# Starting the weight conversion one attention round sooner in a fused attention, SwiGLU and maxout kernel

## The chip, the cores and the metric

The kernel runs on one core of a Trainium2 chip, as one program. The metric is the device time of one execution in microseconds (us). Engine names are those of the profile: PE is TensorE's matmul, PEld its weight load, DVE VectorE, ACT ScalarE, POOL GpSimd, SP SyncE, which here only issues DMAs. A "q" behind an engine (SPq) is its instruction queue.

## What is computed

Three layers follow one another. The first is a causal attention with a decay, over 2 batches, 8 heads, 768 positions and head size 64, in blocks of 64 with a running state:

```
Dmask     = lam ** (i - j)            for i >= j, else 0
intra     = ((qb @ kb.T) * Dmask) @ vb
inter     = (qb * lam ** (i + 1)) @ kv_state
kv_state  = lam ** 64 * kv_state + (kb * lam ** (63 - j)).T @ vb
```

The second layer takes the result as 1536 tokens of 512 features, normalises them (RMS), and computes `(silu(xn @ w_gate) * (xn @ w_val)) @ w_out` with 1536 hidden features. The third computes `maximum(x @ w1, x @ w2, x @ w3) @ w_out2` with 768 hidden features. The weight matrices arrive as 64-bit floats, so every weight is read as two 32-bit words.

## The kernel before, in words

**Weights.** The weights are cut into units of 128 hidden features. `load_to` (L164) loads one unit as raw words: a 512 KB transfer into the tile `wraw`, issued on SP as three DMAs for the gate and value matrices (`crosswise`, L119) and as one for the others. `begin_unit` (L231) then makes two ACT instructions of it: the absolute value of the high words into the tile `W` (L253) and a shift of the low words inside `wraw` (L254). `words_of_unit` (L204) turns these into a 32-bit float with three DVE instructions (L209, L212, L216) and one POOL add (L219). `finish_unit` (L174) splits the result into a high part `wh` (ACT, L180) and a low remainder `wl` (POOL, L183). A product is three matmuls: high by high, low by high, high by low. `W` has three buffers in the pool `wp`, and one more in a later pool for some units of the third layer. `wraw` has three buffers in `wp` and two in the pool `ld`.

**Order of the units.** `unit_list` (L128) begins g0 v0 g1 v1 g2 o0 o1 v2 g3 v3 o2 o3, where g, v and o are gate, value and output matrix and the number is the block of hidden features. These twelve are the units for which there is room while the attention runs.

**Attention.** The 1536 tokens are twelve chunks of 128. Seven rounds s = 0 to 6 (the loop at L985) run the steps of `attn_q` in the order of `orders` (L435). In round s the letter T is `turn` of chunk s (transposes `pk`, `pq`, their copies `kT`, `qT` on ACT, the scaled queries `qs` on DVE, which need `lami`), C is `scores` of chunk s-1 (which needs the decayed keys `kd`, made on POOL from `Tm`), a and b are the masked scores `A` (DVE, from `Tm`), V advances the state `S`, M is `mixed` of chunk s-2 (`px` on PE, then `sq` and `x` on ACT), U sums the squares (`pm` on PE, `ms` on DVE, `ri` on POOL), N applies the norm (`pb`, `x`, `xh`), R makes `xl` (POOL). T also issues the next loads: value of chunk s+1, key and query of chunk s+2 (L104), each 256 KB in pieces of 256 bytes.

Between these steps stand the weights. At the end of rounds 2 to 6 one raw unit is loaded (L1010), and at the end of rounds 3 to 6 one unit is begun (L1012); the round after a unit was begun makes its words, and the round after that finishes it. So when `first_stage` (L649) starts, g0 is finished, v0 and g1 have their words, and v1 has been begun. Everything is in one hand-written order, and every engine works through its own instructions in that order: an ACT instruction that waits for a DMA holds up all ACT instructions behind it.

**After the rounds.** `first_stage` runs the second layer on the first four hidden blocks while the rest of the attention is spread over its gaps. `hidden1` (L614) computes gate and value product of one hidden block for 512 tokens; `out_two` (L631) multiplies two finished hidden blocks with o0 and o1, four output tiles of six matmuls each. In the gaps, `third_of_unit` (L259) carries the unit pipeline on by one third of a unit. When the attention is through, the other hidden blocks and the third layer follow, as sums and differences of products.

**Set-up.** L970 to L981: `diag` is a doubled identity; eight scans make `Tm` (the mask of every head), two copies make `lamh`, and four scans make `lami` (the powers of lambda that scale queries and state).

Of the kernel before, what the change touches and what calls it, by code (L numbers as in the profile page):

```python
# [9 lines left out]
F32 = mybir.dt.float32  # L10
F32R = mybir.dt.float32r
AF = mybir.ActivationFunctionType
ALU = mybir.AluOpType
PSUM = bass.MemoryType.PSUM

I32 = mybir.dt.int32
U32 = mybir.dt.uint32

P = 128
# [7 lines left out]
def tile_decay_attention_swiglu_maxout(  # L27
# [16 lines left out]
    nc = tc.nc  # L44
    B, H, S, D = q.shape
    NT, DM = out.shape
    NP = H // 2
# [5 lines left out]
    C = P // 2  # L53
# [8 lines left out]
    wp = ctx.enter_context(tc.tile_pool(name="wp", bufs=WBUFS))  # L62
    psum = ctx.enter_context(tc.tile_pool(name="psum", bufs=8, space=PSUM))
    att_ctx = ctx.enter_context(ExitStack())
    attc = att_ctx.enter_context(tc.tile_pool(name="attc", bufs=1))
# [3 lines left out]
    lates = []  # L69
# [5 lines left out]
    lam8 = attc.tile([P, H], F32, name="lam8")  # L75
    lamh = attc.tile([P, NP], F32, name="lamh")
    g_sb = attc.tile([P, KD], F32, name="g_sb")
    ones = attc.tile([P, P], F32, name="ones")
    ident = attc.tile([P, P], F32, name="ident")
    zeros = attc.tile([P, P], F32, name="zeros")  # L80
    mhalf = attc.tile([P, 1], F32, name="mhalf")
# [13 lines left out]
    def loads_to(c):  # L95
        while nxt_load[0] <= min(c, NCH):
            n = nxt_load[0]
            if n:
                load(n - 1, 2)
            load(n, 0)  # L100
            load(n, 1)
            nxt_load[0] += 1
# [61 lines left out]
    def load_to(n):  # L164
        while pos["load"] < min(n, len(raw_list)):
            nm, f = raw_list[pos["load"]]
            more = pos["load"] % 5 > 2 and pos["load"] < 3 * PLAIN - 2
            t = (ld if more else wp).tile([P, KD, 2 * P], I32, tag="raw", name="wraw", bufs=2 if more else 3)
            for to, src in crosswise(t, source[nm](f)) if nm in "gv" else [(t, source[nm](f))]:
                nc.sync.dma_start(out=to, in_=src)  # L170
            raws[nm, f] = t
            pos["load"] += 1
# [58 lines left out]
    def begin_unit():  # L231
        if pos["made"] == len(unit_list):
            return
        key = unit_list[pos["made"]]
        at = group_of[key] % 2
        if first_use[key] <= pos["step"] + 6 and at < len(wpools) and (key is None or room[at]):
            pos["made"] += 1
            if key is None:
                stage1.append((None,) * 5)
                return  # L240
            room[at] -= 1
            held[key] = at
            if key[0][0] == "T":
                stage1.append((key, None if second_sum(key) else words[key[0][1], key[1]], at, None, None))
                return
            load_to(pos["raw"] + (3 if pos["half"] else 1))
            pos["raw"] += 1
            t = raws.pop(key).rearrange("p k (f w) -> p (k f) w", w=2)
            lo, hi = t[:, :, 0], t[:, :, 1]
            spare = key[0] in "12" and key[1] % 2  # L250
            W = (lates[0] if spare else wp).tile([P, 512], I32, tag="W", name="W", bufs=1 if spare else 3)
            words[key] = W
            nc.scalar.activation(out=W.bitcast(F32), in_=hi.bitcast(F32), func=AF.Abs)  # L253
            nc.scalar.activation(out=lo, in_=lo.bitcast(U32), func=AF.Copy, scale=2.0 ** -29)  # L254
            stage1.append((key, W, at, lo, hi))
# [87 lines left out]
    last_state = [None]  # L343

    def next_state(c, h, old):
        S_ = att.tile([P, NP, D], F32, tag="S", name="S", bufs=4)
        pS = st[c]["sc"][h][:, HF:].rearrange("p (a e) -> p a e", e=D)
        if old is None:
            nc.vector.tensor_copy(out=S_, in_=pS)
        else:  # L350
            for a in range(NP):
                nc.vector.scalar_tensor_tensor(out=S_[:, a, :], in0=old[:, a, :], scalar=lami[:, a, C - 1:C], in1=pS[:, a, :],
                                               op0=ALU.mult, op1=ALU.add)
        return S_

# [26 lines left out]
    def mixed(c):  # L382
        for part in range(2):
            half_mixed(c, part)
        px = st[c]["px"]
        sq = att.tile([P, NP, P], F32, tag="sq", name="sq", bufs=1)
        x = att.tile([P, NP, P], F32, tag="x", name="x", bufs=3)
        for n in range(2):
            nc.scalar.activation(out=sq[:, 2 * n:2 * n + 2, :], in_=px[n][:, :2, :], func=AF.Square)
        for a in range(NP):  # L390
            nc.scalar.activation(out=x[:, a, :], in_=px[a // 2][:, a % 2, :], func=AF.Copy, scale=g_sb[:, a:a + 1])
        ss = sq
        if c > CPNB:
            ss = att.tile([P, 1, P], F32, tag="ss", name="ss", bufs=1)
            nc.vector.tensor_reduce(out=ss[:, 0, :], in_=sq.rearrange("p a t -> p t a"),
                                    axis=mybir.AxisListType.X, op=ALU.add)
        st[c] = dict(x=x, ss=ss)

    def summed(c):
        d = st[c]  # L400
        pm = bank("pm")
        n = d["ss"].shape[1]
        for a in range(n):
            nc.tensor.matmul(out=pm[:, 0:1], lhsT=d["ss"][:, a, :], rhs=ones[:, 0:1], start=a == 0, stop=a == n - 1)
        ms = att.tile([P, 1], F32, tag="ms", name="ms")
        nc.vector.tensor_scalar(out=ms, in0=pm[:, 0:1], scalar1=1.0 / DM, scalar2=EPS, op0=ALU.mult, op1=ALU.add)
        ri = att.tile([P, 1], F32, tag="ri", name="ri")
        nc.gpsimd.tensor_tensor(out=ri, in0=ms, in1=mhalf, op=ALU.pow)
        d["ri"] = ri

# [546 lines left out]
    with tc.manual_schedule():  # L957
        nc.scalar.dma_start(out=lam8, in_=lam.rearrange("(o h) -> o h", o=1).to_broadcast([P, H]))
        loads_to(0)
        for to, src in crosswise(g_sb, rms_g.rearrange("(a p) -> p a", p=P)):  # L960
            nc.scalar.dma_start(out=to, in_=src)
        make_identity(nc, ident)
        nc.vector.memset(ones, 1.0)
        nc.vector.memset(zeros, 0.0)
        nc.scalar.activation(out=mhalf, in_=zeros[:, 0:1], func=AF.Silu)
        nc.vector.memset(mhalf, -0.5)
        warm = bank("warm")
        for i in range(9):
            nc.tensor.matmul(out=warm[:, 0:P], lhsT=zeros, rhs=zeros, start=True, stop=True)
        nc.vector.tensor_tensor(out=diag, in0=ident[:, :C], in1=ident[:, C:], op=ALU.add)  # L970
        for h in range(H):
            nc.vector.tensor_tensor_scan(
                out=Tm[:, h, :], data0=lam8[:, h:h + 1].to_broadcast([P, C]), data1=diag,
                initial=0.0, op0=ALU.mult, op1=ALU.add)
        for hf in range(2):
            nc.vector.tensor_copy(out=lamh[64 * hf:64 * hf + 64, :],
                                  in_=lam8.rearrange("p (a t) -> p t a", t=2)[64 * hf:64 * hf + 64, hf, :])
        for a in range(NP):
            nc.vector.tensor_tensor_scan(
                out=lami[:, a, :], data0=lamh[:, a:a + 1].to_broadcast([P, C]), data1=zeros[:, :C],  # L980
                initial=1.0, op0=ALU.mult, op1=ALU.add)  # L981
        loads_to(1)
        pos["narrow"] = False
        unit_ = None
        for s_ in range(CPNB + 3):  # L985
            if stage1:
                unit_ = stage1.pop(0)
            while attn_q[0][0] == s_:
                fn = attn_q[0][1]
                attn_step()  # L990
                if unit_ and s_ == CPNB + 2:
                    if fn is named["U"][1]:
                        words_of_unit(3, *added_later)
                    elif fn is named["V"][1]:
                        for n in range(3):
                            words_of_unit(n, *unit_, split_add=True)
                        split_unit.append(unit_)
                        stage2.append(unit_[:3])
                elif unit_ and fn is named["b"][1]:
                    words_of_unit(0, *unit_)  # L1000
                elif unit_ and fn is named["U"][1]:
                    words_of_unit(1, *unit_)
                    if stage2:
                        finish_unit(*stage2.pop(0))
                elif unit_ and fn is named["V"][1]:
                    words_of_unit(2, *unit_, split_add=s_ == CPNB + 1)
                    added_later = unit_
                    stage2.append(unit_[:3])
            if s_ > 1:
                load_to(pos["load"] + 1)  # L1010
            if s_ > 2:
                begin_unit()  # L1012
        finish = first_stage()
        pos["step"] = len(steps)
        second_stage(finish)
# [31 lines left out]
```

## Time and profile before

| | us |
|---|---|
| median of three runs | 548.31 |
| lowest and highest run | 547.35, 548.59 |
| the profiled execution, its own time | 547.73 |
| its span, first to last instruction | 545.9 |
| PE busy | 531.4 |
| DVE, ACT, POOL busy | 374.2, 280.1, 300.9 |

Times of single instructions are counted from the start of the span. In a line of a timeline the first number is the start and the second the length, "x4" the number of merged instructions, and the bracket the idle time of that engine just before, with what ended it. [...]

### The profile page before, as it was taken

The numbers are of one execution on the slowest core, as the hardware profiler recorded it, in microseconds if no ns is written. First come the engines' busy times: TensorE is split into PE (matmuls) and PEld (weight loads), VectorE is DVE, ScalarE is ACT, GpSimd is POOL, SyncE is SP. The second block draws the span as 40 slices with busy tenths as digits, with TensorE's granted clock in tenths as the row PEclk, the third lists the DMA queues.
The fourth block names the chain that finished last, engine by engine and source line by source line (L and its number), as shares of the span: only waits on it lengthen the run. The fifth ranks groups of instructions, "written<-read, shape, count | busy, mean of one in ns | idle before, by whom it ended". The sixth has DMA issues, their size and how long they took to land.

```text
span 545.9 us, 9739 instructions
## 1 busy us (share of the span) xinstructions
PE 531.4 (97%) x3728; PEld 438.8 (80%) x3728; DVE 374.2 (69%) x680; ACT 280.1 (51%) x541; POOL 300.9 (55%) x247
## 2 busy tenths in 40 slices
PE   7799979999999999999999999999999999999997
PEld 6677758788888888888888888888888888888886
DVE  5676777635977677768677575887777477684464
ACT  3585674436364655464447426646466755651120
POOL 2366887441426377385566646896287554962050
PEclk9978989999999999999999999999999999999999
DMA  8886852200202132131231221121123222200015
GB/s 189 214 209 193 206 138 73 67 1 0 78 0 76 41 116 75 42 115 45 73 90 63 79 66 51 41 77 40 38 78 116 82 78 74 85 33 0 0 45 187
DMA packets 65598, 44.67 MB, mean 82 GB/s; under 512 B 40080, under 2 KB 61840, under 8 KB 65552
## 3 DMA queue, kind: packets, MB, share of 16 engines
q1 hardware_dynamic: 64848, 44.05, 27.9%
q8 instruction: 29, 0.48, 0.4%
q14 instruction: 17, 0.14, 0.1%
q10 hardware_dynamic: 704, 0.01, 0.1%
HBM read 40.90 MB, written 3.15 MB: 81 GB/s over the span
## 4 chain that ended last, share of the span: by engine, by line
PE 85%; POOL 5%; issue 4%; DMA 2%; ACT 1%; DVE 1%; SPq 1%; POOLq 0%; ACTq 0%; DVEq 0%
PE p L684 32%; PE acc L875 9%; PE r L684 8%; PE acc L483 6%; PE acc L481 6%; PE acc L482 6%; PE pv L491 5%; PE pg L491 5%; PE q L684 4%; DMA wraw<-in_moe_w_gate_dram 2%; PE px L378 2%; POOL W L219 2%; POOL wl L183 1%; SPq L170 1%; POOL hl L502 1%
## 5 line engine op out<-in xcount | busy, mean ns | idle before, releaser
L183 POOL TENSOR_TENSOR wl<-W,wh 128x512 fp32r<-128x512 f32 x77 | 100.7, 1308 | 62.9 <-ACT wh L180 60.5
L219 POOL TENSOR_TENSOR W<-W,wraw 128x512 int32<-128x512 int32 x60 | 80.6, 1344 | 70.8 <-DVE W L216 66.5
L180 ACT CAST wh<-W 128x512 fp32r<-128x512 f32 x77 | 47.8, 621 | 77.4 <-POOL W L219 77.3
L502 POOL TENSOR_TENSOR hl<-sg,hh 128x512 fp32r<-128x512 f32 x36 | 47.2, 1310 | 32.0 <-ACT hh L501 32.0
L481 PE MATMUL acc<-hh,wh 128*128 128x512 f32 x144 | 57.3, 398 | 1.9 <-ACT wh L180 1.9
L483 PE MATMUL acc<-hh,wl 128*128 128x512 f32 x144 | 57.0, 396 | 0.6 <-POOL wl L183 0.6
L684 PE MATMUL p<-xl,wh 128*128 128x512 f32 x148 | 57.6, 389 | 0.0
L684 PE MATMUL p<-xh,wh 128*128 128x512 f32 x148 | 57.6, 389 | 0.0
L684 PE MATMUL p<-xh,wl 128*128 128x512 f32 x148 | 57.6, 389 | 0.0
L482 PE MATMUL acc<-hl,wh 128*128 128x512 f32 x144 | 56.6, 393 | 0.0
L253 ACT ACTIVATE W<-wraw 128x512 f32<-128x512 f32 x60 | 40.4, 673 | 19.5 <-POOL wl L183 10.8
L839 DVE TENSOR_TENSOR acc_sb<-acc,acc_sb 128x512 f32<-128x512 f32 x46 | 31.7, 690 | 19.3 <-PE acc L483 18.1
L209 DVE TENSOR_SCALAR mid<-W 128x512 f32<-128x512 f32 x58 | 39.7, 685 | 3.4 <-ACT W L253 3.4
L212 DVE TENSOR_SCALAR mid<-mid 128x512 int32<-128x512 int32 x58 | 40.2, 693 | 0.8
L216 DVE SCALAR_TENSOR_TENSOR W<-wraw,mid 128x512 int32<-128x512 int32 x58 | 39.5, 682 | 1.4
L254 ACT ACTIVATE wraw<-wraw 128x512 int32<-128x512 uint32 x60 | 39.9, 665 | 0.0
L739 ACT COPY c<-p 128x512 f32<-128x512 f32 x34 | 19.9, 587 | 37.9 <-PE p L684 37.9
L502 POOL TENSOR_TENSOR hl<-m,hh 128x512 fp32r<-128x512 f32 x18 | 24.2, 1350 | 23.0 <-ACT hh L501 22.9
L684 PE MATMUL p<-yh,wl 128*128 128x512 f32 x90 | 35.0, 389 | 0.0
L684 PE MATMUL p<-yh,wh 128*128 128x512 f32 x90 | 35.0, 389 | 0.0
L684 PE MATMUL p<-yl,wh 128*128 128x512 f32 x90 | 35.0, 389 | 0.0
L481 PEld LDWEIGHTS acc<-hh,wh 128*128 128x128 f32 x144 | 27.5, 191 | 7.6 <-ACT wh L180 2.0
(176 smaller groups left out, 1319.7 us busy)
## 6 DMA issues: line engine op xcount, KB each, us to landing
wraw<-in_moe_w_out_dram SPq DMA_DIRECT2D x18, 512.0 KB, 3.4
wraw<-in_moe_w_dram SPq DMA_DIRECT2D x18, 512.0 KB, 3.5
kn<-in_k_dram SPq DMA_DIRECT2D x12, 256.0 KB, 4.5
qn<-in_q_dram SPq DMA_DIRECT2D x12, 256.0 KB, 4.8
vn<-in_v_dram SPq DMA_DIRECT2D x12, 256.0 KB, 4.6
wraw<-in_moe_w_gate_dram SPq DMA_DIRECT2D x12, 256.0 KB, 3.0
wraw<-in_moe_w_gate_dram SPq DMA_DIRECT2D x24, 128.0 KB, 3.2
wraw<-in_moe_w_val_dram SPq DMA_DIRECT2D x12, 256.0 KB, 2.9
```

The costliest lines, as they stand in the source:

```text
L180: nc.scalar.copy(out=wh, in_=W.bitcast(F32))
L183: nc.gpsimd.tensor_tensor(out=wl, in0=W.bitcast(F32), in1=wh.bitcast(F32), op=ALU.subtract)
L212: nc.vector.tensor_scalar(out=mid[key], in0=mid[key], scalar1=0x07FFFFFF, scalar2=3, op0=ALU.bitwise_and, op1=ALU.logical_shift_left)
L219: nc.gpsimd.tensor_tensor(out=W, in0=W, in1=lo, op=ALU.add)
L253: nc.scalar.activation(out=W.bitcast(F32), in_=hi.bitcast(F32), func=AF.Abs)
L481: nc.tensor.matmul(out=out, lhsT=wh, rhs=xh_, start=first, stop=False)
L482: nc.tensor.matmul(out=out, lhsT=wh, rhs=xl_, start=False, stop=False)
L483: nc.tensor.matmul(out=out, lhsT=wl, rhs=xh_, start=False, stop=last)
L491: nc.tensor.matmul(out=ps, lhsT=w[:, kk * P:(kk + 1) * P], rhs=x[:, kk, :], start=n == 0, stop=n == len(todo) - 1)
L502: nc.gpsimd.tensor_tensor(out=dst_l, in0=src, in1=dst_h.bitcast(F32), op=ALU.subtract)
L684: nc.tensor.matmul(out=ps, lhsT=w[:, ks], rhs=r[:, o + k, :], start=first and k == 0 and n == 0, stop=k == 1 and n == 2, skip_group_check= ...
L875: nc.tensor.matmul(out=acc[:, cs], lhsT=x[:, ts], rhs=w[:, cs], start=n == 0, stop=n == len(todo) - 1)
```

## The change

One raw unit is loaded at the end of rounds 1 to 6 instead of 2 to 6, and one unit is begun at the end of rounds 2 to 6 instead of 3 to 6. `W` gets four buffers in `wp`, and the buffer in the later pool goes. The space comes from smaller attention tiles: `ones` keeps one column, the state `S` three buffers instead of four, the summed squares `ss` use the tile `zeros`, and `ms` and `ri` use columns of `diag`. In the set-up the copies `lamh` and the scans of `lami` move ahead of the scans of `Tm`.

```diff
-    ones = attc.tile([P, P], F32, name="ones")
+    ones = attc.tile([P, 1], F32, name="ones")
...
-            spare = key[0] in "12" and key[1] % 2
-            W = (lates[0] if spare else wp).tile([P, 512], I32, tag="W", name="W", bufs=1 if spare else 3)
+            W = wp.tile([P, 512], I32, tag="W", name="W", bufs=4)
...
-        S_ = att.tile([P, NP, D], F32, tag="S", name="S", bufs=4)
+        S_ = att.tile([P, NP, D], F32, tag="S", name="S", bufs=3)
...
-            ss = att.tile([P, 1, P], F32, tag="ss", name="ss", bufs=1)
+            ss = zeros.rearrange("p (a t) -> p a t", a=1)
...
-            nc.tensor.matmul(out=pm[:, 0:1], lhsT=d["ss"][:, a, :], rhs=ones[:, 0:1], start=a == 0, stop=a == n - 1)
-        ms = att.tile([P, 1], F32, tag="ms", name="ms")
+            nc.tensor.matmul(out=pm[:, 0:1], lhsT=d["ss"][:, a, :], rhs=ones, start=a == 0, stop=a == n - 1)
+        ms = diag[:, c % 2:c % 2 + 1]
...
-        ri = att.tile([P, 1], F32, tag="ri", name="ri")
+        ri = diag[:, 2 + c % 2:3 + c % 2]
...
-        for h in range(H):
-            nc.vector.tensor_tensor_scan(
-                out=Tm[:, h, :], data0=lam8[:, h:h + 1].to_broadcast([P, C]), data1=diag,
-                initial=0.0, op0=ALU.mult, op1=ALU.add)
         for hf in range(2):
             nc.vector.tensor_copy(out=lamh[64 * hf:64 * hf + 64, :],
...
         for a in range(NP):
             nc.vector.tensor_tensor_scan(
                 out=lami[:, a, :], data0=lamh[:, a:a + 1].to_broadcast([P, C]), data1=zeros[:, :C],
                 initial=1.0, op0=ALU.mult, op1=ALU.add)
+        for h in range(H):
+            nc.vector.tensor_tensor_scan(
+                out=Tm[:, h, :], data0=lam8[:, h:h + 1].to_broadcast([P, C]), data1=diag,
+                initial=0.0, op0=ALU.mult, op1=ALU.add)
         loads_to(1)
...
+            if s_:
+                load_to(pos["load"] + 1)
             if s_ > 1:
-                load_to(pos["load"] + 1)
-            if s_ > 2:
                 begin_unit()
```

## Rows read from the trace of the kernel before

**Rows 1.** The page's 40 equal slices of the span: PE's busy share in tenths.

```profile
PE   7799979999999999999999999999999999999997
```

**Rows 2.** Stretches: length, then busy us of PE, PEld, DVE, ACT, POOL; clock, DMA, GB/s.

```profile
60.00:70.00 10.00, 9.27 (x160) 6.66 (x159) 7.59 (x18) 7.19 (x17) 9.65 (x9) 1.00 0.75 191
70.00:80.00 10.00, 7.62 (x58) 5.74 (x58) 7.21 (x19) 7.18 (x14) 7.91 (x8) 0.83 0.56 159
```

**Rows 3.** Timeline of PE: the first output products, transposes, then `px` of chunk 8.

```profile
68.82 0.39 PE L483 MATMUL acc<-hh,wl 128*128 128x512 f32 x1
69.49 0.35 PE L404 MATMUL pm<-ones,ss 128*128 128x1 f32 x2 [0.28 <-DVE ss L395]
71.76 0.50 PE L481 MATMUL acc<-hh,wh 128*128 128x512 f32 x1 [1.91 <-ACT wh L180]
...
73.11 0.79 PE L483 MATMUL acc<-hh,wl 128*128 128x512 f32 x1 [0.62 <-POOL wl L183]
...
77.50 0.39 PE L483 MATMUL acc<-hh,wl 128*128 128x512 f32 x1
77.73 0.60 PE L298 MATMUL pk<-ident,kn 128*128 128x128 f32 x4
...
79.40 0.46 PE L378 MATMUL px<-qs,S 64*64 64x64 f32 x16
```

**Rows 4.** Timeline of POOL, from the remainder of o0 to that of o1.

```profile
66.28 1.28 POOL L183 TENSOR_TENSOR wl<-W,wh 128x512 fp32r<-128x512 f32 x1
...
68.78 1.29 POOL L502 TENSOR_TENSOR hl<-sg,hh 128x512 fp32r<-128x512 f32 x1
71.78 1.28 POOL L183 TENSOR_TENSOR wl<-W,wh 128x512 fp32r<-128x512 f32 x1 [1.72 <-ACT wh L180]
```

**Rows 5.** Timeline of ACT: three begun units, and the high part of o1.

```profile
24.15 0.68 ACT L253 ACTIVATE W<-wraw 128x512 f32<-128x512 f32 x1 [2.16 <-DMA wraw<-in_moe_w_gate_dram]
...
29.76 0.68 ACT L253 ACTIVATE W<-wraw 128x512 f32<-128x512 f32 x1 [1.31 <-DMA wraw<-in_moe_w_val_dram]
...
35.87 0.68 ACT L253 ACTIVATE W<-wraw 128x512 f32<-128x512 f32 x1 [0.77 <-DMA wraw<-in_moe_w_gate_dram]
...
71.09 0.61 ACT L180 CAST wh<-W 128x512 fp32r<-128x512 f32 x1
```

**Rows 6.** Timeline of PE, the last sum of the rounds and the first gate product.

```profile
38.23 1.31 PE L404 MATMUL pm<-ones,sq 128*128 128x1 f32 x8 [0.79 <-ACT x L391]
39.41 0.77 PE L491 MATMUL pg<-xh,wh 128*128 128x512 f32 x1
```

**Rows 7.** Timeline of SP: issues of one weight unit in the rounds, and one much later.

```profile
17.40 2.34 SPq L170 DMA_DIRECT2D wraw<-in_moe_w_gate_dram  x3
...
29.40 3.35 SPq L170 DMA_DIRECT2D wraw<-in_moe_w_gate_dram  x3
...
39.20 2.09 SPq L170 DMA_DIRECT2D wraw<-in_moe_w_gate_dram  x3
...
140.33 1.68 SPq L170 DMA_DIRECT2D wraw<-in_moe_w_val_dram  x3
```

**Rows 8.** Stretches as in rows 2: one of the rounds, then two of 2 us.

```profile
24.00:30.00 6.00, 5.09 (x150) 4.64 (x143) 4.23 (x13) 4.55 (x12) 2.33 (x4) 0.89 0.88 223
...
40.00:42.00 2.00, 2.00 (x35) 1.26 (x33) 1.75 (x4) 1.32 (x3) 1.79 (x3) 0.50 0.89 227
...
44.00:46.00 2.00, 2.00 (x40) 1.25 (x42) 1.84 (x3) 1.25 (x6) 0.00 (x0) 0.57 0.90 341
```

**Rows 9.** Scans of Tm and of lami: ns min/median/max; then POOL's first decayed keys.

```profile
L972 DVE TENSOR_TENSOR_SCAN Tm<-lam,diag x8: 265/269/291, 5.1 to 6.4; 128x64 f32<-128x64 f32 x8
...
L979 DVE TENSOR_TENSOR_SCAN lami<-lamh,zeros x4: 259/645/1094, 6.9 to 9.0; 128x64 f32<-128x64 f32 x4
...
6.71 2.08 POOL L288 TENSOR_TENSOR kd<-kn,Tm 128x512 f32<-128x512 f32 x2 [5.40 <-DVE Tm L972]
```

**Rows 10.** Timeline of DVE, second half of the masked scores of chunk 8.

```profile
75.12 0.42 DVE L334 TENSOR_TENSOR A<-sc,Tm 128x256 f32<-128x256 f32 x1
```

## The prediction, on record before the changed kernel was run

> **What bounds the kernel now.** I read the page first. In its 40 slices of 13.6 us PE is nine tenths busy or more from the seventh slice on, down to the last one, the output; the low digits stand in the first, second and sixth [rows 1]. So behind 82 us PE sets the pace, and the end moves only as far as the PE work ahead of that point moves. The stretches of 10 us say where PE falls short late in that part: 9.27 us busy from 60 to 70, and 7.62 from 70 to 80, there with a granted clock of 0.83 on the mean [rows 2].
>
> Then the timeline of PE in that hole. The third matmul of the first output tile starts at 68.82. The sum of squares `pm` behind it waits 0.28 for DVE, the next matmul 1.91 for the high part of o1, and the second one after that 0.62 for its low part; the transposes `pk` of the next chunk come at 77.73 [rows 3]. [...] Without the two waits for o1, and at that pace, the stretch would be 0.23, then 0.44 to the start of `pm`, 0.35 for it, and 15 times 0.23: `pk` at 68.82 + 0.23 + 0.44 + 0.35 + 3.45 = 73.29. The hole costs 77.73 - 73.29 = 4.44 us, of which 2.53 are the two waits and the rest is mostly the clock, which fell while PE waited.
>
> Why o1 is late: its high part is cast on ACT at 71.09 [rows 5], its remainder on POOL from 71.78 to 73.06 [rows 4], just ahead of the matmul that needs it at 73.11. The unit before it, o0, had its remainder 5.5 us sooner, at 66.28 [rows 4]. POOL is 9.65 of 10 us busy just before [rows 2].
>
> Last, what sets the start of the first stage. In the rounds ACT begins three units, and at each it stood still for the raw words: 2.16, 1.31 and 0.77 us [rows 5]. Behind such a wait stand ACT's `sq` and `x` of the next round; for `x` PE's last `pm` of the rounds waited 0.79, and the first gate product follows at 39.41 [rows 6]. The raw words come late since SP issues without a pause: a unit's three issues take 2.34 and 3.35 in the rounds, 1.68 when nothing else is loaded [rows 7], and a typical round moves 223 GB/s at a DMA share of 0.88 [rows 8].
>
> **The change part by part.**
>
> *Units one round sooner, the gain.* No instruction is added; one unit's work (three DVE, two POOL, three ACT instructions) moves from the first stage into the rounds. In the order of each engine every later unit then stands where its forerunner stood: o1's remainder stands where o0's did, at 66.28 plus 1.28 = 67.56, ahead of its use at about 70. The two waits and the low clock behind them go: -4.44. What is late next: the low half of the second hidden block is done by POOL at 68.78 + 1.29 = 70.07 [rows 4], and PE would want it at 69.84 + 0.23 = 70.07, no wait. `px` follows `pk` by 79.40 - 77.73 = 1.67 [rows 3], so it would come at 74.96, but its masked scores end on DVE at 75.12 + 0.42 = 75.54 [rows 10], in a queue that PE's haste doesn't shorten: 0.58 comes back. Gain 4.44 - 0.58 = 3.86.
>
> *The same, the cost.* One raw unit goes into SP's queue ahead of values of chunk 3, keys and queries of chunk 4, and all that follow. They and each later unit land by one unit's issue later than that slot did before, while ACT asks for each unit at the same place of its order as it asked for the one before. So each of the gates at `W` comes later by that amount, and with it `sq`, `x`, `pm` and the start of the first stage. In the rounds such an issue took 2.34, 3.35 and, the last of five, 2.09 [rows 7]. The unit that counts is the one begun last under a wait; I take 2.09, the row nearest to that end of the rounds. Bounds: 0, if lighter moments of the queues take it up, and 3.35. ACT's and POOL's extra work in the rounds lies in the same waits. Behind the new first wait on ACT stand `sq`, `x` and `xh` of the round, then `kT` and `qT`; PE waits for these, which is the cost just counted.
>
> [...]
>
> [...]
>
> *Scans.* The eight scans of `Tm` took 265 to 291 ns each; of the four of `lami`, alike in size, the dearest took 1094, while POOL made two decayed keys for 2.08 [rows 9]. Ahead of the keys all twelve should cost about 270, and DVE is through some 1.5 us sooner; but the first keys, which need `Tm`, start about 1.1 later (four scans of 0.27). PE's first scores wait for the keys, the masks for both: the one pays for the other, and the gate of the third round covers what is left. 0, bounds -0.5 and +1.1.
>
> *Fourth buffer of W.* It takes the wait for the third unit before it off ACT. The cast behind that wait needs POOL's add anyway: 0, bounds 0 and -1.28, one remainder [rows 4]. In the third layer four buffers stand where three and one stood: 0.
>
> *Small tiles.* `S` with three buffers: the tile that it reuses was last read by `mixed`, which stands ahead of it on PE. `ss`, `ms`, `ri`, `ones` in other places: the same instructions, and their last readers lie a round back. 0 for all.
>
> **Sum**: -3.86 + 2.09 - 0.5 = -2.27. From the profiled execution's 547.73 that is 545.46; that execution lies 0.58 under the median of the runs, 548.31, to which the forecast is put: 546.0.
>
> **The rivals.**
>
> 1. *The queue takes the load up.* The cost of the extra load is nil; the gain stays: -3.86, 544.4. For it: the waits at the gates shrink from 2.16 to 0.77, so the loads catch up with the rounds [rows 5]. Against: they never vanish while units are begun under a wait. Chance 0.16.
> 2. *The hole moves.* PE that comes 4 us sooner meets POOL, which was 9.65 of 10 us busy [rows 2], at the next keys, norms or remainders; half the gain, 1.9, is lost. -2.27 + 1.9 = -0.4: 547.9, no change. Against: after 80 us, units stand ready before PE asks, now by one place more. 0.20.
> 3. *The gates cost more than the hole* (slower). The wait for raw words now stands in one round more, and ACT's in-order queue hands it to PE there too; the slips add up to two units' issues, 2.34 + 3.35 = 5.69 [rows 7]. Then -3.86 + 5.69 = +1.83: 550.1. It decides once the first gate product starts later than 39.41 + 3.86 = 43.3. For: three gates in a row in the rows; against: rounds without a wait have slack between `sq` and `pm`. 0.14.
> 4. *The change doesn't do what it says*: the unit is begun sooner in the order, but its words land so late that o1 is no sooner; start and hole cancel: 548.3. 0.04.
>
> **How the numbers follow.** The forecast has 0.46, with a range of its own from 544.8 to 547.2 (unit issue 0.9 to 3.3 instead of 2.09). Over 0.2%, 1.1 us, is about what a measurement of this kernel can tell from no change. Faster: 0.42 of the forecast, 0.16, and 0.02 of rival 2: 0.60. Within: 0.04 of the forecast, 0.16 of rival 2, 0.04: 0.24. Slower: 0.14 and 0.02 of rival 2: 0.16. The range goes from 543.8 (rival 1 without the 0.58 at `px`) to 549.2; it leaves out most of rival 3 and a little below.
>
> **What would show it.** The first gate product at 41.5 (39.41 plus 2.09); waits at four gates; the `lami` scans all near 270 ns; no wait for o1's parts and no clock under 1 between 70 and 80; about 0.6 of a wait at `px` of chunk 8; behind 82 us everything alike, only earlier by 2. A start at 39.5 is rival 1; new waits of PE between 70 and 100 are rival 2; a start after 43.3 is rival 3. The prediction is wrong if the hole stays with o1 ready, or if the start slips by more than a unit's issue.

## The result and the profile after

**Slower.** The changed kernel takes 552.32 us (median; 549.96 to 555.8) beside 547.83 of the kernel before in the same session: ratio 1.0094, 95% interval 1.0065 to 1.0124. The forecast was 546.0, its range ended at 549.2. The profiled execution of the changed kernel took 550.88, 1.4 under that median, with a span of 549.1 us, 3.2 more than before. (The kernel before has its own median in each set of runs, 545.6 to 547.8, so every ratio below is against the runs of its own set. Lines behind the change have other numbers in the changed kernel: L480 is L481 of before, L297 is L298.)

First the timeline of PE in the changed kernel: the first gate product, the start of the output products, and from there on every wait up to the transposes `pk` of chunk 11.

```profile
42.69 0.50 PE L490 MATMUL pg<-xh,wh 128*128 128x512 f32 x1
...
70.48 0.40 PE L480 MATMUL acc<-hh,wh 128*128 128x512 f32 x1
...
71.62 0.35 PE L403 MATMUL pm<-ones,zeros 128*128 128x1 f32 x2 [0.29 <-DVE zeros L394]
...
75.61 0.60 PE L297 MATMUL pk<-ident,kn 128*128 128x128 f32 x4
...
77.33 0.50 PE L480 MATMUL acc<-hh,wh 128*128 128x512 f32 x1 [0.68 <-DVE W L216]
...
83.54 0.63 PE L321 MATMUL sc<-qT,kT 64*64 64x64 f32 x27 [1.48 <-ACT x L390]
...
91.81 0.63 PE L297 MATMUL pk<-ident,kn 128*128 128x128 f32 x4 [1.88 <-DMA kn<-in_k_dram]
...
93.03 0.63 PE L299 MATMUL pq<-ident,qn 128*128 128x128 f32 x4 [0.59 <-DMA qn<-in_q_dram]
...
106.52 0.60 PE L297 MATMUL pk<-ident,kn 128*128 128x128 f32 x4
```

The hole of [rows 3] is gone: no wait for o1. But behind it stand four waits that the kernel before does not have, 4.63 us together. The next two `pk` of the kernel before:

```profile
88.90 0.60 PE L298 MATMUL pk<-ident,kn 128*128 128x128 f32 x4
...
103.03 0.60 PE L298 MATMUL pk<-ident,kn 128*128 128x128 f32 x4
```

The stages, from the two timelines:

| stage, us | before | after | difference | forecast |
|---|---|---|---|---|
| start to first gate product | 39.41 | 42.69 | +3.28 | +2.09 |
| to `pk` of chunk 9 | 38.32 | 32.92 | -5.40 | -4.94 |
| to `pk` of chunk 10 | 11.17 | 16.20 | +5.03 | +0.58 |
| to `pk` of chunk 11 | 14.13 | 14.71 | +0.58 | 0 |
| to the end of the span | 442.87 | 442.58 | -0.29 | 0 |
| sum | 545.9 | 549.1 | +3.20 | -2.27 |

So the gain came, and a little more; the miss of 5.47 us is 4.45 between chunks 9 and 10, 1.19 at the start and small change. The timeline of ACT shows the four gates, the places where ACT waits for raw words before it begins a unit (4.81 at the first, 9.4 together, before 4.24 in three [rows 5]), and, much later, a cast that waits for POOL ahead of the `sq` and `x` for which PE stood still at 83.54:

```profile
20.65 0.69 ACT L252 ACTIVATE W<-wraw 128x512 f32<-128x512 f32 x1 [4.81 <-DMA wraw<-in_moe_w_gate_dram]
...
27.41 0.67 ACT L252 ACTIVATE W<-wraw 128x512 f32<-128x512 f32 x1 [2.45 <-DMA wraw<-in_moe_w_val_dram]
...
33.68 0.70 ACT L252 ACTIVATE W<-wraw 128x512 f32<-128x512 f32 x1 [1.46 <-DMA wraw<-in_moe_w_gate_dram]
...
39.31 0.67 ACT L252 ACTIVATE W<-wraw 128x512 f32<-128x512 f32 x1 [0.68 <-DMA wraw<-in_moe_w_val_dram]
...
81.79 0.62 ACT L180 CAST wh<-W 128x512 fp32r<-128x512 f32 x1 [1.61 <-POOL W L219]
82.32 0.65 ACT L388 ACTIVATE sq<-px 128x256 f32<-128x256 f32 x2
82.86 1.15 ACT L390 ACTIVATE x<-px,g_sb 128x128 f32<-128x128 f32 x4
```

Why the keys of chunk 10 came late shows in SP's own timeline. Changed kernel, then the kernel before:

```profile
70.99 1.69 SPq L170 DMA_DIRECT2D wraw<-in_moe_w_gate_dram  x3
86.06 1.67 SPq L170 DMA_DIRECT2D wraw<-in_moe_w_val_dram  x3
87.83 0.54 SPq L92 DMA_DIRECT2D kn<-in_k_dram  x1
```

```profile
74.35 1.69 SPq L170 DMA_DIRECT2D wraw<-in_moe_w_gate_dram  x3
76.14 0.54 SPq L92 DMA_DIRECT2D kn<-in_k_dram  x1
...
90.36 1.68 SPq L170 DMA_DIRECT2D wraw<-in_moe_w_val_dram  x3
92.14 0.54 SPq L92 DMA_DIRECT2D kn<-in_k_dram  x1
```

The load of raw words at 86.06 (the 14th unit, v4) was issued once the tile that it reuses had come free: the trace puts SP's wait before it, 11.0 long, down to POOL's add (L219), and that add ends at 86.04:

```profile
84.72 1.32 POOL L219 TENSOR_TENSOR W<-W,wraw 128x512 int32<-128x512 int32 x1 [0.97 <-DVE W L216]
```

In the kernel before, the keys of chunk 10 stood ahead of that load (76.14), and those of chunk 11 behind it. One unit sooner in the order, the load stands ahead of chunk 10, and its keys, which could have gone at about 72.8 (70.99 + 1.69 and a step), go at 87.83.

Last the page, of the kernel before and of the changed one: the transfers on the main queue as a share of 16 engines' span, and the median time of an issue to its landing for keys and for a raw weight.

```profile
q1 hardware_dynamic: 64848, 44.05, 27.9%
...
kn<-in_k_dram SPq DMA_DIRECT2D x12, 256.0 KB, 4.5
...
wraw<-in_moe_w_val_dram SPq DMA_DIRECT2D x12, 256.0 KB, 2.9
```

```profile
q1 hardware_dynamic: 64848, 44.05, 30.1%
...
kn<-in_k_dram SPq DMA_DIRECT2D x12, 256.0 KB, 5.5
...
wraw<-in_moe_w_val_dram SPq DMA_DIRECT2D x12, 256.0 KB, 2.9
```

The same packets and bytes take more engine time, and only keys, queries and values land later (queries 5.7 after 4.8, values 5.3 after 4.6), not the weights. The diff doesn't touch those transfers, only their place and what else stands in the queue: as I read the program, tiles lie one behind the other, and with `ones` of one column the tiles behind it begin, by my estimate, 32 bytes past a multiple of 256 instead of on one. No view shows these addresses. The place became the second suspect.

The scans did what the forecast says: the four of `lami` now take 0.84 together (5.29), and the first masked scores start about where they did (9.53, before 9.74).

### The profile page after: what moved, and what is told of

Its sections match the earlier page's. It is cut to its first block, busy times and chain, and to the rows that moved or that the text cites. A ratio compares the mean times of both kernels' runs of the same rounds, so it can differ in the third digit from the quotient of the medians.

```text
span 549.1 us, 9738 instructions
## 1 busy us (share of the span) xinstructions
PE 531.6 (97%) x3728; PEld 438.7 (80%) x3728; DVE 371.7 (68%) x680; ACT 279.5 (51%) x541; POOL 301.2 (55%) x247
## 3 DMA queue, kind: packets, MB, share of 16 engines
q1 hardware_dynamic: 64848, 44.05, 30.1%
HBM read 40.90 MB, written 3.15 MB: 80 GB/s over the span
## 4 chain that ended last, share of the span: by engine, by line
PE 87%; DMA 4%; SPq 2%; issue 2%; ACT 2%; POOL 1%; DVE 1%; ACTq 0%; POOLq 0%; DVEq 0%
PE p L683 34%; PE acc L874 9%; PE r L683 8%; PE acc L480 6%; PE acc L481 6%; PE acc L482 6%; PE pv L490 5%; PE pg L490 5%; PE q L683 4%; DMA wraw<-in_moe_w_val_dram 2%; DMA qn<-in_q_dram 2%; PE px L377 2%; SPq L92 1%; SPq L170 1%; POOL W L219 1%
## 5 line engine op out<-in xcount | busy, mean ns | idle before, releaser
L219 POOL TENSOR_TENSOR W<-W,wraw 128x512 int32<-128x512 int32 x60 | 80.6, 1344 | 70.2 <-DVE W L216 65.9
L480 PE MATMUL acc<-hh,wh 128*128 128x512 f32 x144 | 56.7, 394 | 0.7 <-DVE W L216 0.7
L481 PE MATMUL acc<-hl,wh 128*128 128x512 f32 x144 | 56.2, 390 | 0.0
L212 DVE TENSOR_SCALAR mid<-mid 128x512 int32<-128x512 int32 x58 | 40.2, 693 | 0.8
L216 DVE SCALAR_TENSOR_TENSOR W<-wraw,mid 128x512 int32<-128x512 int32 x58 | 39.5, 681 | 1.1
L500 ACT CAST hh<-sg 128x512 fp32r<-128x512 f32 x36 | 22.3, 619 | 23.0 <-DVE sg L624 17.0
```

Of the source, the lines that this page charges most:

```text
L212: nc.vector.tensor_scalar(out=mid[key], in0=mid[key], scalar1=0x07FFFFFF, scalar2=3, op0=ALU.bitwise_and, op1=ALU.logical_shift_left)
L219: nc.gpsimd.tensor_tensor(out=W, in0=W, in1=lo, op=ALU.add)
L480: nc.tensor.matmul(out=out, lhsT=wh, rhs=xh_, start=first, stop=False)
L481: nc.tensor.matmul(out=out, lhsT=wh, rhs=xl_, start=False, stop=False)
```

## The experiments

Theory: two losses that beginning sooner need not bring, the load that blocks SP's queue and the place of the tiles, hide what it does; beginning sooner itself gains the hole and loses part of it again. Rivals: the gates alone make it slower; or the moved scans do. The next four ran together, with 545.84 for the kernel before.

**e1, the 14th load held back** (changed kernel; the load waits until the attention is through):

```diff
-            load_to(pos["raw"] + (3 if pos["half"] else 1))
+            ahead = pos["raw"] + (3 if pos["half"] else 1)
+            load_to(ahead if lates else min(ahead, 13))
```

> The changed kernel, with the fourteenth raw unit (v4) not loaded before the attention is through. Theory: in the changed kernel SP waits with that load for a buffer until 86.06, and keys and queries of chunk 10 stand behind it; PE waits 1.88 and 0.59 for them. Held back, the keys are issued near 73, both waits go, and the time is 2.5 to 2.9 under the changed kernel's median of 552.3: about 549.6. Rival: the keys only share the delay of ACT and POOL in front of them; the waits turn up at the next use, and the time stays within 1 of the changed kernel.

Measured: 548.54, ratio 1.0046 [1.0029, 1.0062], 0.48% under the changed kernel's. SP's timeline has the keys of chunk 10 ahead of the load again, and in PE's the transposes wait for nothing:

```profile
71.27 1.80 SPq L170 DMA_DIRECT2D wraw<-in_moe_w_gate_dram  x3
73.17 0.54 SPq L92 DMA_DIRECT2D kn<-in_k_dram  x1
...
86.33 1.68 SPq L170 DMA_DIRECT2D wraw<-in_moe_w_val_dram  x3
```

```profile
83.81 0.63 PE L322 MATMUL sc<-qT,kT 64*64 64x64 f32 x27 [1.47 <-ACT x L391]
...
90.03 0.60 PE L298 MATMUL pk<-ident,kn 128*128 128x128 f32 x4
```

The queue is shown to be one cause, about half of the loss. The wait for `x` stays.

**e2, the scans alone** (kernel before with the scans of `lami` ahead of those of `Tm`, as in the change's diff):

> The kernel before, with the scans of lami and the copies ahead of those of Tm, nothing else. Theory: the scans no longer share their time with POOL's keys (four in 0.8 instead of 2.4 us), the keys start 1.0 later, and the first rounds come out alike; the time is that of before within 1. Rival: the later keys push every round: 1.0 to 1.5 slower.

Measured: 545.91, 0.9999 [0.9977, 1.0022]. The scans are worth nothing either way, as forecast.

**e3, the raw load alone** (kernel before, units begun as before):

```diff
-            if s_ > 1:
+            if s_:
                 load_to(pos["load"] + 1)
```

> The kernel before, with each raw unit loaded one round sooner but begun where it was. Theory: the gates cost because the changed kernel asks for each unit a round sooner than its words can come; a load alone moves nothing that ACT waits for, so the three waits of 2.16, 1.31 and 0.77 shrink, the first gate product comes at 38.5 to 39.5, and the time is that of before or up to 1 less; the hole at o1 stays. Rival: keys and queries behind the extra load hold the rounds up, the start slips by 2 or more and so does the time.

Measured: 543.95, 0.9961 [0.9946, 0.9976], faster than before. On ACT none of the four gates waits any more (the first and the last of them), on PE the hole stays:

```profile
22.14 0.70 ACT L253 ACTIVATE W<-wraw 128x512 f32<-128x512 f32 x1
...
38.22 0.70 ACT L253 ACTIVATE W<-wraw 128x512 f32<-128x512 f32 x1
```

```profile
68.41 0.50 PE L481 MATMUL acc<-hh,wh 128*128 128x512 f32 x1 [1.91 <-ACT wh L180]
69.76 0.80 PE L483 MATMUL acc<-hh,wl 128*128 128x512 f32 x1 [0.62 <-POOL wl L183]
```

So the part of the change that I had charged with 2.09 us gains 0.39%, 2.1 us, when it stands alone. Nor is it this load that makes the keys of chunk 10 late: here its `pk` waits for nothing and follows 11.15 behind that of chunk 9 (85.37 after 74.22), as in the kernel before (11.17). Part of the gain may be the clock that TensorE was granted (a share; the highest in these traces is 1.00): in this trace it is 1.00 from 12 to 52, in that of the kernel before 0.58 from 28 to 32 and 0.50 from 40 to 44. But e2, which isn't faster, has 1.00 up to 40 too, and its gate product at 40.90 lasts 0.39, against 0.63 at 40.41 in the kernel before.

**e4, the changed kernel with raw loads from round 0:**

```diff
-            if s_:
-                load_to(pos["load"] + 1)
+            load_to(pos["load"] + 1)
```

> The changed kernel, with the raw loads yet one round sooner (from round 0). Theory: the four waits at the gates (4.81, 2.45, 1.46, 0.68) go to under 0.5 each, the first gate product comes at 40 to 41 instead of 42.69, and the time is about 2 under the changed kernel: 550.3. Rival: SP's stream is full from the first us, keys and queries of the early rounds now come late instead, and the start stays at 42.5 or later.

Measured: 549.65, 1.0067 [1.0048, 1.0085]. The gates are 0.58, then nothing, but PE waits 1.65 for queries at 14.94 instead: with keys and queries that land this late (5.3 and 5.7 us), a still earlier weight seems to take their place (e11 below, with the tiles aligned, has no such wait). The wait of 1.86 for the keys of chunk 10 stays.

The second set asks about the place of the tiles (kernel before: 546.05).

**e5, the changed kernel with its tiles back on multiples of 256 bytes** (`ones` takes 64 columns and is read as one):

```diff
-    ones = attc.tile([P, 1], F32, name="ones")
+    ones = attc.tile([P, 64], F32, name="ones")
...
-            nc.tensor.matmul(out=pm[:, 0:1], lhsT=d["ss"][:, a, :], rhs=ones, start=a == 0, stop=a == n - 1)
+            nc.tensor.matmul(out=pm[:, 0:1], lhsT=d["ss"][:, a, :], rhs=ones[:, 0:1], start=a == 0, stop=a == n - 1)
```

> The changed kernel with ones 64 columns wide instead of 1 (one column is used), which puts the key, query and value tiles back on multiples of 256 bytes; in the changed kernel they start 32 bytes past one. Theory: the pieces of 256 bytes cost the DMA engines more there; on multiples of 256 the main queue's share goes back from 30.1% to about 28%, a key's landing from 5.5 to about 4.6 us, the first gate product from 42.7 to about 41.3, and the time is 1 to 2 under the changed kernel's. Rival: the loads are slower only because raw weights stand among them; share, landing and time stay as in the changed kernel.

Measured: 548.27, 1.0044 [1.0024, 1.0064], 0.50% under the changed kernel's. The page:

```profile
q1 hardware_dynamic: 64848, 44.05, 27.9%
...
kn<-in_k_dram SPq DMA_DIRECT2D x12, 256.0 KB, 4.3
```

**e6, the same with 16 columns**, so that the tiles lie 64 bytes past a multiple of 256:

> The same with ones 16 columns wide: the tiles start 64 bytes past a multiple of 256. [...]

Measured: 552.49, 1.0116 [1.0094, 1.0138], no better than the changed kernel; queue share 29.4%, keys 5.0. A shift by 64 bytes is no better than one by 32.

**e7, the kernel before, shifted by 32 bytes** and otherwise untouched:

```diff
-    ones = attc.tile([P, P], F32, name="ones")
+    ones = attc.tile([P, P + 8], F32, name="ones")
```

> The kernel before with ones 8 columns wider, which puts its key, query and value tiles 32 bytes past a multiple of 256; nothing else. Theory: the main queue's share rises from 27.9% to about 30%, the rounds, which wait for raw words, stretch, the first gate product comes at 40.5 to 41.5, and the time is 1 to 2 above that of before. Rival: the place of a tile costs nothing: within 0.5.

Measured: 549.25, 1.0069 [1.0046, 1.0092], 0.69% or 3.8 us: about twice the upper end of what I expected. The first gate product comes at 43.44, also later than expected. The page has the changed kernel's signs without any of its other edits:

```profile
q1 hardware_dynamic: 64848, 44.05, 29.3%
...
kn<-in_k_dram SPq DMA_DIRECT2D x12, 256.0 KB, 5.2
...
wraw<-in_moe_w_val_dram SPq DMA_DIRECT2D x12, 256.0 KB, 3.0
```

All tiles behind `ones` move in this run, the operands of the engines too. But up to 120 us DVE, ACT and POOL work on them at the same pace (mean of one: `A` 418 ns before and 417 here, `x` 383 and 385, `kd` 1061 and 1062), while PE's `pq` waits 2.2 for queries, before for none, and POOL's `kd` 3.4 for keys, before 1.8. The price shows at the transfers, not at these engines.

**e8, units not sooner in the rounds but denser behind them** (changed kernel, aligned, 14th load held, units begun from round 3 as before; the pauses between thirds of a unit dropped up to the 17th gap):

```diff
-        if not lates and (pos["half"] - 1) % 4:
+        if not lates and ((pos["half"] - 1) % 4 or 1 < pos["half"] < 17):
```

> A version built from what the runs have shown: raw loads one round sooner, units begun where the kernel before begins them, four W buffers, tiles on multiples of 256, the fourteenth raw unit held back, and three more thirds of a unit in the first gaps of the first stage, so that the pipeline is a unit ahead when o1 is needed. Theory: start near 37.5 without a gate, the hole at o1 gone, the same small waits for DVE and ACT after it: 541 to 543. Rival: the earlier thirds hold up the attention's instructions on ACT and POOL; the hole goes, but PE waits as much elsewhere: 544 or more, as with the sooner loads alone.

Measured: 547.73, 1.004 [1.0021, 1.0059]. A miss; the rival came: `pb` waits 1.62 for POOL's `xl` at 52.29, and the waits for `W` (0.74) and `x` (1.42) are there as well. The weights' steps are not free between those of the attention.

The third set takes both side losses out (kernel before: 545.67).

**e9, aligned and held: e5 and e1 together.**

> The changed kernel with both suspected losses taken out at once: its attention tiles on multiples of 256 bytes again, and the 14th raw unit held back until the attention is through. Theory (the two are separate and all there is): aligned alone was 1.0044 of before and holding the load back is worth 0.48% (550.88 to 548.3 in the profiled executions), so 0.9996, bounds 0.998 to 1.001; engine share of the key/value queue 27.9%, no wait at the transposes of chunk 10, which come at 87 (aligned 88.90 less 1.18 and the 0.83 behind it). Rival 1 (the two are the same loss: late keys, cured by either): 1.004. Rival 2 (beginning sooner gains once nothing else is lost, as I forecast): 0.996.

Measured: 545.56, 0.9994 [0.9978, 1.0009]. The two losses add up: 0.50% and 0.48% alone, 1.00% together.

**e10, the same with units begun from round 3:**

```diff
-            if s_ > 1:
+            if s_ > 2:
                 begin_unit()
```

> As the run before it in this set, but units are begun from round 3 on again, as in the kernel before; raw loads from round 1, four buffers of W, the small tiles, the scans and the held load stay. The difference of the two prices beginning one round sooner alone. Theory (beginning sooner gives back at the gates and at DVE and ACT what it gains in the hole): this one is at 0.996 to 0.997 of before, like the raw load from round 1 alone (0.9961), so beginning sooner costs 0.3 to 0.4%; all gates at nothing, first gate product at 37.4, the hole at o1 there again. Rival (as I forecast, the hole is worth more than the gates): this one is slower than the run before it by 0.2% or more. Rival 2: four buffers of W and the small tiles cost something themselves: 0.999 or more.

Measured: 544.34, 0.9976 [0.9956, 0.9996]. Beginning sooner makes 0.18% of difference, for the worse, with intervals that overlap; the expected 0.3 to 0.4% is not shown, and it nets about nothing. PE's timelines say how. e9:

```profile
72.57 0.60 PE L298 MATMUL pk<-ident,kn 128*128 128x128 f32 x4
...
74.30 0.50 PE L481 MATMUL acc<-hh,wh 128*128 128x512 f32 x1 [0.69 <-DVE W L216]
...
80.51 0.63 PE L322 MATMUL sc<-qT,kT 64*64 64x64 f32 x27 [1.48 <-ACT x L391]
...
86.74 0.60 PE L298 MATMUL pk<-ident,kn 128*128 128x128 f32 x4
```

and e10, with the hole and without those two waits:

```profile
69.04 0.50 PE L481 MATMUL acc<-hh,wh 128*128 128x512 f32 x1 [1.91 <-ACT wh L180]
...
70.41 0.79 PE L483 MATMUL acc<-hh,wl 128*128 128x512 f32 x1 [0.63 <-POOL wl L183]
...
75.06 0.60 PE L298 MATMUL pk<-ident,kn 128*128 128x128 f32 x4
...
86.22 0.60 PE L298 MATMUL pk<-ident,kn 128*128 128x128 f32 x4
```

From first gate product (39.38 and 38.03) to `pk` of chunk 9 e9 takes 33.19 and e10 37.03: 3.84 gained. From there to chunk 10 they take 14.17 and 11.16: 3.01 given back.

**e11, e9 with raw loads from round 0** (e4's edit):

> Changed kernel, aligned, 14th load held back, and raw loads from round 0, so that the units begun one round sooner find their words. Theory (the gates are what eats the gain of the hole): all gates at nothing or under 1, first gate product 38 to 39, no hole at o1, transposes of chunk 10 at 85 to 86, time 0.994 to 0.996 of before. Rival (the raw load of round 0 takes the first keys' and queries' place, and PE waits in rounds 0 and 1 instead): first gate product at 40, 0.998 to 1.000.

Measured: 543.03, 0.9955 [0.9936, 0.9973]. One wait of 0.41 is left at the gates, and with the words there in time the same begun units are faster than the kernel before. That beginning sooner is worth something of its own this doesn't show: the intervals of e3 and e10, with units begun as before, overlap with this one. The stretch from chunk 9 to 10 still takes 14.15.

**e12, the kernel before with raw loads from round 0:**

> The kernel before with raw loads from round 0 instead of round 2, nothing else. From round 1 on gave 0.9961 with all gates at nothing, so there is nothing left for a still earlier load to take away. Theory (a load counts only where a gate waits for it): 0.996 to 0.998, never under 0.995, with a new wait for the queries of chunk 1 or 2 of 1 to 2 in the first rounds. Rival (it gains by taking load off the later rounds too): 0.993 or less, first gate product under 36.5.

Measured: 544.97, 1.0005 [0.9978, 1.0033], not the gain of e3, and worse than expected, though the ends of the two intervals nearly meet. The twelve runs go from 543.87 to 551.17 us; the two longest have a granted clock of 0.978, the others 0.990 to 0.997. The wait for queries did not come; in the trace PE's second half of the scores waits 1.90 at 24.00 for something the profile doesn't name (0.91 at 23.74 in the kernel before). Why is open.

The last set (kernel before: 545.63) asks what gives the 3.0 us back. The suspect is the cast on ACT, at 81.79 in the changed kernel, that waits for POOL ahead of `sq` and `x`.

**e13, e11 with that step later:**

```diff
-        if not lates and (pos["half"] - 1) % 4:
+        if not lates and ((pos["half"] - 1) % 4 or pos["half"] == 29) and pos["half"] != 27:
```

> The best kernel so far (aligned, 14th load held back, raw loads from round 0, units begun from round 2) with one third of a weight's work moved from the 27th gap to the 29th, so that on ACT the cast of its high part stands behind the squares and x of chunk 8 instead of ahead of them. Theory (the cast, waiting 1.6 for POOL's add, is what holds the scores of chunk 9 up by 1.48): the wait at the scores goes or falls under 0.4, the transposes of chunk 10 come 1.2 to 1.7 sooner after those of chunk 9 (12.5 to 12.9 instead of 14.15), and the time falls from 0.9955 to 0.993 of before. Rival (DVE, which sums the squares and makes the queries for the same chunk, or POOL hold it up anyway): a wait of over 1 for DVE or POOL takes its place, 0.995 to 0.996.

By the edit nothing is done at the 27th gap, and the 29th, a pause until now, does a third. The thirds keep their order, so the cast's third goes from the 27th to the 28th gap and the one behind it from the 28th to the 29th: one gap each, not two for one of them.

Measured: 541.32, 0.993 [0.9906, 0.9955], the time expected, and the stretch a little shorter still. On ACT `sq` and `x` now come ahead of the cast, which waits for nothing; on PE the scores of chunk 9 have no wait, and `pk` of chunk 10 follows 12.35 behind that of chunk 9 (69.96):

```profile
74.40 0.70 ACT L389 ACTIVATE sq<-px 128x256 f32<-128x256 f32 x2
74.94 1.19 ACT L391 ACTIVATE x<-px,g_sb 128x128 f32<-128x128 f32 x4
76.13 0.62 ACT L180 CAST wh<-W 128x512 fp32r<-128x512 f32 x1
```

```profile
71.66 0.50 PE L481 MATMUL acc<-hh,wh 128*128 128x512 f32 x1 [0.67 <-DVE W L216]
...
82.31 0.60 PE L298 MATMUL pk<-ident,kn 128*128 128x128 f32 x4
```

**e14, the step ahead of it moved as well** (26 instead of 27 in e13's edit, so that three thirds come one gap later):

> As the run before it, but the third ahead of it (which begins the next unit, two ACT instructions) goes from the 26th gap to the 29th, and the cast with it to the next gap after. Theory: as there for the scores, and the wait of the output product for DVE (0.68) stays, since that one belongs to the unit before; 0.993 to 0.994. Rival (every third put off makes a later unit late): the gate or output products behind 85 wait for a weight by 0.5 or more, 0.995 or more.

Measured: 542.0, 0.9934 [0.9913, 0.9955]; 12.39 from chunk 9 to 10. The wait for DVE at the output product, which I expected to stay, goes, and two waits of 0.33 and 0.53 at `px` take its place. No gain over e13.

e13 is the fastest kernel here: 0.7% under the kernel before, 1.6% under the changed one by the two ratios. Its interval just parts from that of e10 (0.9956 to 0.9996) and overlaps with that of e3 (0.9946 to 0.9976), the sooner raw loads alone.

## Why the prediction was wrong

**Failed: "small tiles, 0 for all".** I asked of `ones` only who reads it, not what lies behind it. Its new size moved every later tile of the attention, by my estimate by 32 bytes against a multiple of 256, and that cost 0.50% (2.7 us; changed kernel against e5), or 0.69% when a shift of 32 bytes was made in the kernel before (e7). Keys, queries and values come in pieces of 256 bytes, and it is their transfers that differ: the queue share is 27.9 to 28.1% unshifted and 29.3 to 30.1% shifted, the landing of keys 4.1 to 4.5 us and 5.0 to 5.5. Why a shifted piece takes longer no run here shows, nor that the unshifted tiles lie on a multiple of 256.

**Failed: the moved loads, followed only through the rounds.** The part on cost says that one raw unit goes into SP's queue "ahead of values of chunk 3, keys and queries of chunk 4, and all that follow", and counts its issue time. It did not ask at each later place whether the load could be issued at all. The 14th unit had to wait for POOL, and chunk 10 stood behind it: 0.48% (e1). What put it there is not the extra load in the rounds, as e3 shows, but the beginning: `begin_unit` issues the load three units ahead, and does so one unit sooner. The fourth `W` buffer, also at 0, wasn't tried alone; e10 has it and is at 0.9976 beside e3's 0.9961, with intervals that overlap.

**Failed in its price: the hole's gain of 3.86.** The hole itself was right: forecast 4.44, at the 0.23 a matmul that PE kept from 77.50 to 77.73 [rows 3] (granted clock 1.00 from 77 to 78), and 3.84 between e9 and e10, whose granted clock is 1.00 from 40 to 50 in both. The wait of 0.58 at `px` did not come; PE waited 0.68 for DVE one step sooner, at the output product, for a weight's words (L216) and not for masked scores. That the two are alike in size is luck. What I left out is the cast of a weight that stands ahead of `sq` and `x` and waits 1.61 for POOL: it holds up the scores by 1.48. e13 shows that this step, the cast with the DVE instruction (L212) of the same third, is the cause: with both behind chunk 8's squares (the two were not taken apart) the wait is gone, the stretch 1.80 shorter (14.15 to 12.35) and the kernel 0.25% under e11 (the two intervals overlap; the stretch is the clearer sign). Of the 3.01 given back, 1.2 remain. My rival 2 had the kind of thing ("PE that comes 4 us sooner meets POOL", half the gain lost): 3.0 of 3.84 were lost, and its chance of 0.20 was too low.

**The start: 2.09 forecast, 3.28 in the trace, and the step not right for either.** e3 has the same extra raw load at the same place and starts sooner, since the words then reach ACT ahead of need; so the load isn't what costs. What costs is that ACT asks a round sooner than the words can be there: with equal loads e9, which asks a round sooner, waits at four gates (4.13, 1.51, 1.04, 0.32), and e10 up to 42 at none. With the tiles aligned the start was at 40.69 and 39.38 (e5, e9), the latter no later than before, and with the tiles shifted alone at 43.44 (e7); so part of the slip is alignment. How much, single traces don't settle: e11, e13 and e14, alike up to there, start at 38.57, 37.22 and 39.08.

**Right:** the scans at 0 (e2); no wait for o1 in the changed kernel; nothing different behind chunk 11 but the shift (442.6 against 442.9). No run shows the clock term of the sum, -0.5; its sign is right. What the runs showed: a granted clock of 0.71 from 40 to 50 before, with 0.50 from 40 to 44 and 0.57 from 44 to 46; 0.83 after, with 1.00 from 40 to 44 and 0.51 from 46 to 48. That may also belong to one execution more than to the kernel: in e2, the kernel before but for the scans, no gate product from 40 to 44 lasts over 0.50, in the kernel before they last 0.63 to 0.77. From first gate product to `pk` of chunk 9 the changed kernel gained 5.40, 1.16 more than the 4.24 that its trace has less between the third output matmul and `pk` of chunk 9 (8.91 of before [rows 3], 75.61 - 70.94 = 4.67 after).

**The rivals.** The outcome has the sign of rival 3, but not its mechanism: it decides from a first gate product at 43.3, and that came at 42.69; the gates, with all else that beginning sooner brings (e9), give 0.9994.

## What to carry to other kernels

When an edit moves one item of a DMA queue that is issued in the order of the program, go on down that queue to its end and ask at each place what the item waits for and which ready load stands behind it: here one load waited 11.0 us, with the keys of chunk 10 behind it. When a tile changes size, look at what lies behind it: here keys, in pieces of 256 bytes, landed in 5.2 us instead of 4.5 once the tiles had moved by 32 bytes (e7). And of a stall that goes, follow each engine's order through the next step of the pipeline, where a cast that waits for another engine (here 1.61 for POOL) may hold up what is due first (the scores, by 1.48).

## What was not expected of the hardware

A shift by 32 bytes that moves the tiles which receive 256-byte pieces costs this kernel 0.69% [0.46, 0.92], with the same instructions, packets and bytes: engine share 27.9% to 29.3%, landing of keys 4.5 to 5.2 us. In the changed kernel a shift by 64 bytes behaves alike (29.4%, 5.0), and one by a whole 256 doesn't pay (27.9%, 4.3). The value weights, in longer pieces, kept a median of 2.9 to 3.1 us in all of them.
